# Residual of a token-mixing block: accumulating DMA into the output against loads and VectorE additions

## The chip, the core and the metric

The kernel runs on one core of one Trainium2 chip. The core has five engines with instruction queues of their own: TensorE (PE in the profile, with its weight loads shown apart as PEld), VectorE (DVE), ScalarE (ACT), GpSimd (POOL) and SyncE (SP). PE writes its results to PSUM; the other data lie in SBUF. DMA transfers between SBUF and the chip's memory are issued from the queues of SP, ACT or POOL and run on 16 DMA engines. The metric is device time in microseconds of one execution, given as the median of several runs.

## The reference, cut to what matters

```python
def reference(A_x, A_wqkv, A_wo, B_x, B_w1, B_b1, B_w2, B_b2):
    ...
    def _B_ref(x, w1, b1, w2, b2):
        h = _layernorm(x, axis=-1)
        u = jnp.einsum("bsd,sf->bdf", h, w1) + b1
        u = _gelu(u)
        y = jnp.einsum("bdf,fs->bds", u, w2) + b2
        return y.transpose(0, 2, 1)

    x = A_x
    h = x + _A_ref(_layernorm(x, axis=-1), A_wqkv, A_wo)
    h2 = h + _B_ref(_layernorm(h, axis=-1), B_w1, B_b1, B_w2, B_b2)
    return h2
```

_A_ref, left out here, is linear attention with 32 heads and a product with wo. The input is bf16 with S = 2048 tokens and D = 1024 channels. The first half adds linear attention to x and gives h. The second half mixes over the tokens: a product with w1 (2048 x 3584), a gelu, a product with w2 (3584 x 2048), a bias per token. Its result is added to h, the residual. This last addition, h + mixer, is what the change is about.

## The kernel before

The kernel has three stages. Attention runs up to about 235 us: projections, the key-value products, then for each of the NS = 16 blocks of 128 tokens the output projection (out_mm), which yields a block of h as a 128x1024 tile. out_evac (L1393) copies that block to SBUF as h_bf, takes its statistics for the layer norm, and stores it to a scratch tensor in memory, h_dram[i] (L1402). The normalized h stays in SBUF as the input of the mixer's first product; the plain h is needed again only at the very end.

The first mixer product (class Mixer1) and the second (class Mixer2) follow, the latter from about 390 us. Both use a seven-product scheme of Strassen's kind: instead of eight block products, seven products of sums and differences of blocks (methods p1 to p7) are accumulated in PSUM, and some of the seven are themselves taken apart once more in the same way (class Inner, methods i1 to i7). PE does the products; DVE makes the sums and differences of operands (tiles sa, is, gi, gs) and of partial results (e); ACT copies between PSUM tiles. psA, psB and psC are PSUM tiles of 128x512, psI one of 128x256.

A Mixer2 object with number p makes the blocks 2p and 2p + 1 of 128 tokens (sh = 0 or 1), each in two halves of CW = 512 channels (dh = 0 or 1). That gives 32 results of 128x512. Two Mixer2 objects at a time form a Quad, handled by run2, which interleaves the matmuls of one Quad with those that end the Quad before it: steps p4 of the earlier pair (result sh = 1, dh = 0) are filled in between the inner products of the next. The order of PE and DVE in this part is written out by hand: all instructions there keep program order (Held.on = True).

A result ends in Mixer2.out (L472). First either ACT (evac, from psA, psC or e) or DVE (evac_shared, from psC or psB with e added) writes the result with its bias to ot, an SBUF tile with three buffers. Then DVE adds hr, the block of h that fetch (L467) loaded from h_dram earlier, and SP stores ot to the output. hr has six buffers, and its 32 loads and the stores share SP's queue with the loads of w2 (load_w2, L160). [...]

The last Quad is called with cut = 384: the very last result is split into 384 and 128 columns (split), so that the work behind the last matmul is short.

Of the kernel before, what the change touches and what calls it, by code (L numbers as in the profile page):

```python
# [10 lines left out]
P = 128  # L11
F32 = mybir.dt.float32
BF16 = mybir.dt.bfloat16
FP16 = mybir.dt.float16
ACT = mybir.ActivationFunctionType
ALU = mybir.AluOpType
# [6 lines left out]
BANK = 512  # L23
XRL = 3
XR2 = 8
ACT_SET_LN_EXP = 6
SEED_RESIDUAL = True

# [2 lines left out]
def kernel(  # L31
# [12 lines left out]
    nc = tc.nc  # L44
    x = A_x.flatten_outer_dims()
    o_dram = out.flatten_outer_dims()
    S, D = x.shape
    F = B_w1.shape[1]
    NS, ND, NF = S // P, D // P, F // P
    CW = min(BANK, D)  # L50
# [147 lines left out]
            part()  # L198

    dram = ctx.enter_context(tc.tile_pool(name="dram", bufs=1, space=bass.MemoryType.DRAM))  # L200
    h_dram = [dram.tile([P, D], BF16, name=f"h_dram{i}") for i in range(NS)]
    sactx = ctx.enter_context(ExitStack())
    mctx = ctx.enter_context(ExitStack())

# [26 lines left out]
    dve, pe, act = Held(nc.vector), Held(nc.tensor), Held(nc.scalar, key="scalar")  # L231
    hv, ht, hs, hd = (Held(e, True) for e in (nc.vector, nc.tensor, nc.scalar, nc.sync))
# [222 lines left out]
    class Mixer2(Product7):  # L455
# [9 lines left out]
            return dve.tensor_tensor(t, self.a11, self.a21, ALU.subtract)  # L465

        def fetch(self, sh, dh):  # L467
            t = outp.tile([P, CW], BF16, tag="hr", bufs=6, name="hr")
            nc.sync.dma_start(t[:], h_dram[2 * self.p + sh][:, dh * CW:(dh + 1) * CW])
            self.hr[sh, dh] = t  # L470

        def out(self, sh, dh, a, b, op):  # L472
            i = 2 * self.p + sh
            ot = outp.tile([P, CW], BF16, tag="ot", bufs=3, name="ot")
            op(ot[:, a:b], b2_sb[:, i:i + 1])
            dve.tensor_tensor(ot[:, a:b], ot[:, a:b], self.hr[sh, dh][:, a:b], ALU.add)
            nc.sync.dma_start(o_dram[i * P:(i + 1) * P, dh * CW + a:dh * CW + b], ot[:, a:b])

        def evac(self, sh, dh, ps, a=0, b=CW):
            self.out(sh, dh, a, b, lambda ot, bias: nc.scalar.activation(  # L480
# [12 lines left out]
    def share(sts):  # L493
        t = cpool.tile([P, 2, BANK], F32, tag="e", name="e1")
        for s, st in enumerate(sts):
            st.e = t[:, s, :]
        return t[:]

    class Quad:
# [79 lines left out]
        def run2(self, pend, on_p4, on_p7, cut, third_sums):  # L579
            sts = self.sts  # L580

            def starting():
                self.in1.sums(slice(2, 4))
                self.asums(5)
                self.in5 = self.inner(5)
                self.in5.sums(slice(0, 2))
                sts[0].asum(6)
                for st in sts:
                    st.begin()

            self.interleave(
                self.in1, self.steps(*[st.p4 for st in pend]),
                {"b": starting, "7": lambda: self.in5.sums(slice(2, 4))}, (("b", self.early), ("7", None), ("end", None)),
            )
            sts[1].asum(6)
            on_p4()
            e = share(sts)
            for st in sts:
                st.fetch(1, 1)
            for st in sts:  # L600
                st.fetch(0, 0)
                st.fetch(0, 1)
            sts[0].asum(7)
            self.interleave(self.in5, self.steps(*[st.p6 for st in sts]))
            sts[1].asum(7)
            third_sums()
            self.asums(3)
            in3 = Inner2(sts, 3, self.mov3, "i", self.add_to(e), None)
            in3.sums()
            for st in sts:  # L610
                st.p7()
                dve.tensor_tensor(st.e[:], st.B[:], st.e[:], ALU.add)
            if cut is not None:
                sts[-1].split(cut)
            for st in sts:
                st.fetch(1, 0)
            nxt, halves = on_p7()

            def begin_next():
                if nxt is not None:  # L620
                    nxt.in1 = nxt.inner(1)
                    nxt.in1.sums(slice(0, 2))
                sts[0].evac(0, 1, sts[0].e)

            self.interleave(in3, self.steps(*[st.p2 for st in sts]), {
                "2": halves[0], "7": halves[1], "third": begin_next,
                "end": lambda: self.late.append(lambda: sts[1].evac(0, 1, sts[1].e)),
            }, (("7", None),))
            return sts, nxt
# [111 lines left out]
    with ExitStack() as actx:  # L741
# [21 lines left out]
        with ExitStack() as a1:  # L763
# [256 lines left out]
            def run_step(n, prev, after6=None, after5=None, after7=None, fill=None):  # L1020
# [34 lines left out]
            nc.scalar.add_instruction(  # L1055
                mybir.InstLoadActFuncSet(name=nc.get_next_instruction_name(), act_func_set_id=ACT_SET_LN_EXP, ins=[], outs=[])
            )
# [172 lines left out]
            for q in range(2, NVP):  # L1230
                for R in (KRun, VRun):
                    n = R(q)
                    i = 2 * q + 3 if R is KRun else 2 * q + 4
# [57 lines left out]
        with ExitStack() as a3:  # L1291
# [41 lines left out]
            def den_spread(u):  # L1333
                rows = rd_dram[u].rearrange("(g o h) n -> o h g n", g=4, h=HB)
                for h in range(2):
                    rdb = a3d.tile([P, NH, SW], FP16, tag="rdb", bufs=3, name="rdb")
                    for q in range(HB):
                        hd.dma_start(
                            rdb[q * DH:(q + 1) * DH, :, :],
                            rows[h, q].unsqueeze(0).to_broadcast([DH, 4, SW]),  # L1340
                        )
                    rdbs[u, h] = rdb

            def den(u):
                den_inv(u, den_mm(u))
# [21 lines left out]
            def load_xr(i):  # L1367
                if i < NS:
                    pool = xr2pool if XRL < i <= XRL + XR2 else xrpool
                    xr = pool.tile([P, D], BF16, name="xr")  # L1370
                    hd.dma_start(xr[:], x[i * P:(i + 1) * P, :])
                    xrs[i] = xr
# [20 lines left out]
            def out_evac(i):  # L1393
                ps = seeds.pop(i)
                h_bf = a3w.tile([P, D], BF16, name="h_bf")
                h_bfs[i] = h_bf
                st = a3s.tile([P, NDC, nc.vector.BN_STATS_DIM], F32, name="hst")
                for dc in range(NDC):
                    hs.copy(h_bf[:, dc * CW:(dc + 1) * CW], ps[dc][:, 0:CW])
                    hv.bn_stats(st[:, dc, :], ps[dc][:, 0:CW])  # L1400
                hv.bn_aggr(mv_all[:, i, :], st[:])
                hd.dma_start(h_dram[i][:], h_bf[:])  # L1402

            def h_scale(i):
                lnv = a3s.tile([P, 1], F32, name="hln_l")
# [47 lines left out]
            a3w = a3.enter_context(tc.tile_pool(name="a3w", bufs=4))  # L1453
            xr2pool = a3.enter_context(tc.tile_pool(name="xr2pool", bufs=XR2))

# [7 lines left out]
            for i in range(NS):  # L1463
                seed(i + 1)
                out_mm(i)
                if i == 0:
                    load_xr(XRL + 1)
                    den(NSC - 1)
                    for k in range(XRL + 2, XRL + XR2 + 1):
                        load_xr(k)  # L1470
                if i == 2:
                    den_spread(NSC - 1)
                if i < NS - XRL - XR2 - 1:
                    load_xr(i + XRL + XR2 + 1)
                if i == NS - 1:
# [37 lines left out]
    def next_load1(u):  # L1513
        def load():
            if u < NQ1:
                load_w1(u, 0)
                load_w1(u, 1)
            else:
                first_w2(0)
        return load  # L1520

    def quad1(u):
        return Quad([Mixer1(2 * u), Mixer1(2 * u + 1)], mov1, mov5, mov2, mov3)
# [4 lines left out]
    pend, nxt = cur.run_first(quad1(1), sums1, sums2)  # L1528
    for u in range(1, NQ1):
        cur = nxt  # L1530
        pend, nxt = cur.run1(pend, lambda: quad1(u + 1) if u + 1 < NQ1 else None, next_load1(u + 1), sums3 if u == 1 else None)
# [11 lines left out]
    outp = ctx.enter_context(tc.tile_pool(name="outp", bufs=1, side="right", reuse_waits="tile"))  # L1543
# [46 lines left out]
    def run_all(fs):  # L1590
        for f in fs:
            f()

    def after_p4(u):
        def act():
            run_all(make_t3)
            for p in (2 * u + 2, 2 * u + 3):
                if 4 <= p < NSP:
                    load_w2(p, 1)
        return act  # L1600

    def next2(u):
        for p in (2 * u, 2 * u + 1):
            load_w2(p, 0)
        return quad2(u)

    def after_p7(u):
        return lambda: (next2(u + 1) if 2 * u + 2 < NSP else None, make_t4)

    pend = [cur, Mixer2(1)]  # L1610
    share(pend)
    for st in pend:
        st.fetch(0, 0)
        st.fetch(1, 1)
        st.fetch(0, 1)
    for st in pend:
        if st is pend[1]:
            for m in (5, 6, 7):
                st.asum(m)
            run_all(make_t3_raw)  # L1620
        st.p1()
        st.p5()
        if st is not pend[1]:
            st.p2()
        st.p6()
# [2 lines left out]
    sums5()  # L1628
    for st in pend:
        st.p7()  # L1630
    for st in pend:
        st.fetch(1, 0)
    nxt = next2(1)
    nxt.early = 0
    run_all(make_t4)
# [6 lines left out]
    for u in range(1, NSP // 2):  # L1642
        cur = nxt
        pend, nxt = cur.run2(
            pend, after_p4(u), after_p7(u), CW - P if 2 * u + 2 == NSP else None, sums3 if u == 1 else nop,
        )
# [34 lines left out]
```

## Time and profile before

| What | us |
|---|---|
| median of 5 runs | 563.05 |
| lowest to highest | 562.69 to 563.22 |
| the profiled execution, its own time | 562.69 |
| its span in the profile | 560.9 |
| end of the first part, start of the second mixer product | about 390 |
| start of the last unbroken run of matmuls (42 on psC) | 551.31 |
| last store issued | 558.2 |

The span is what the profiler saw from the first to the last instruction; the execution's own time is 1.8 us more. The profile numbers instructions by line of the source (L229 is a helper through which most of the recorded instructions pass, so the names of tiles tell them apart). In a timeline, a line is a run of like instructions: start, length, engine, line, operation, output and inputs, how many; in brackets stands how long the engine had been idle before, and what it waited for. Matmul ends are modelled, so starts are the safer measure.

The rows of DMA issues that concern the residual, with the size of one and the median time from issue to landing:

```profile
h_dram<-h_bf SPq DMA_DIRECT2D x16, 256.0 KB, 2.0
hr<-h_dram SPq DMA_DIRECT2D x32, 128.0 KB, 2.9
out_dram<-ot SPq DMA_DIRECT2D x31, 128.0 KB, 1.9
```

The core's clock was full throughout (a granted TensorE clock of 1.00 in every stretch).

### The profile page before, as it was taken

What the parts mean: (1) busy time and instruction counts of PE and PEld (TensorE: products, weight loads), DVE (VectorE), ACT (ScalarE), POOL (GpSimd) and SP (SyncE); (2) the same over time, 40 slices, a digit from 0 to 9 for tenths busy, and PEclk for the clock granted to TensorE, in tenths of its full rate; (3) what the DMA queues carried; (4) which work ended last, traced back from release to release, by engine and by line L of the source; (5) the groups of instructions that cost most, each with busy time, mean ns of one, the idle gap of its engine ahead of it and who ended that gap; (6) DMA issues with size and microseconds to landing.
All of it is one profiled execution on the core that took longest, in us unless ns stands there. A gap on an engine that the chain in (4) does not pass through costs nothing.

```text
span 560.9 us, 8720 instructions
## 1 busy us (share of the span) xinstructions
PE 554.0 (99%) x3260; PEld 309.6 (55%) x3276; DVE 447.5 (80%) x853; ACT 288.6 (51%) x611; POOL 1.8 (0%) x8
## 2 busy tenths in 40 slices
PE   8999999999999999999999999999999999999997
PEld 3444444454444444456666766666445655656654
DVE  7898888544776788889989789888998889879874
ACT  5647777756766877645546465564211313313212
POOL 1000000000000000000000000000000000000000
PEclk9999999999999999999999999999999999999999
DMA  9933332115765851103141340422946643642111
GB/s 304 299 74 76 88 82 39 19 56 190 215 192 146 264 178 76 75 1 110 43 150 28 124 151 1 151 70 63 237 134 193 169 110 115 189 134 94 56 39 56
DMA packets 86217, 67.15 MB, mean 120 GB/s; under 512 B 15890, under 2 KB 80160, under 8 KB 86176
## 3 DMA queue, kind: packets, MB, share of 16 engines
q1 hardware_dynamic: 85440, 65.94, 40.2%
q10 hardware_dynamic: 672, 0.66, 0.4%
q8 instruction: 25, 0.41, 0.3%
q14 instruction: 16, 0.13, 0.1%
q0 software_dynamic: 64, 0.01, 0.0%
HBM read 54.54 MB, written 8.91 MB: 113 GB/s over the span
## 4 chain that ended last, share of the span: by engine, by line
PE 91%; DVE 5%; DMA 1%; issue 1%; SPq 0%; ACT 0%; DVEq 0%
PE psI L229 21%; PE acc_t L229 18%; PE psC L229 14%; PE psB L229 8%; PE psC L907 4%; PE psB L907 4%; PE psA L907 4%; PE psA L229 3%; PE psB L341 2%; PE psA L341 2%; PE acc_t L1193 2%; PE psE L907 2%; PE psC L341 2%; PE acc_t L831 2%; DMA x_sb<-in_A_x_dram 1%; PE kvps L860 1%
## 5 line engine op out<-in xcount | busy, mean ns | idle before, releaser
L229 PEld LDWEIGHTS <-is 128*128 128x128 f16 x652 | 63.7, 98 | 29.3 <-issue 0.9
L229 PEld LDWEIGHTS <-sa 128*128 128x128 f16 x606 | 59.3, 98 | 28.3 <-issue 0.4
L229 PEld LDWEIGHTS <-wq 128*128 128x128 bf16 (+1 forms) x503 | 49.2, 98 | 32.9 <-issue 1.0
L229 PE MATMUL acc_t<-wo_sb,pqT 128*128 128x512 f16 x256 | 55.6, 379 | 0.0
L229 PE MATMUL acc_t<-xnT,wq_sb 128*128 128x512 bf16 x188 | 43.1, 379 | 0.2
L229 PEld LDWEIGHTS <-pqT 128*128 128x128 bf16 x256 | 25.0, 98 | 30.5 <-issue 0.6
L191 DVE TENSOR_SCALAR e_sb<-e_sb 128x512 bf16<-128x512 bf16 x64 | 18.5, 290 | 28.8 <-ACT e_sb L187 28.2
L187 ACT ACTIVATE e_sb<-acc_t 128x512 bf16<-128x512 f32 x40 | 23.9, 597 | 24.5 <-PE acc_t L229 12.0
L907 PEld LDWEIGHTS <-xs 128*128 128x128 f16 x208 | 20.0, 98 | 23.4 <-DVE xs L893 1.3
L229 PE MATMUL psC<-gs,wq 128*128 128x512 f16 x140 | 32.0, 379 | 0.0
L229 PE MATMUL psC<-hT,sa 128*128 128x512 f16 x112 | 31.2, 379 | 0.0
L229 PEld LDWEIGHTS <-wq_sb 128*128 128x128 bf16 x192 | 18.5, 98 | 23.0 <-issue 1.3
L229 PE MATMUL psI<-hi,is 128*128 128x256 f16 x200 | 30.0, 273 | 0.0
L229 PE MATMUL psB<-hT,sa 128*128 128x512 f16 x112 | 29.7, 379 | 0.0
L229 DVE BATCH_NORM_STATS2 hst<-acc_t 128x6 f32<-128x512 f32 x32 | 21.4, 692 | 9.1 <-ACT h_bf L229 8.9
L907 PE MATMUL psA<-wkv,xnT 128*128 128x512 bf16 x99 | 26.4, 379 | 0.3
L907 PEld LDWEIGHTS <-xnT 128*128 128x128 bf16 x156 | 15.2, 98 | 18.5 <-issue 0.2
L229 PE MATMUL psC<-hT,wq 128*128 128x512 f16 x96 | 24.6, 379 | 0.0
L229 ACT CAST h_bf<-acc_t 128x512 bf16<-128x512 f32 x32 | 18.4, 581 | 12.0 <-PE acc_t L229 12.0
L229 ACT COPY psI<-psI 128x256 f32<-128x256 f32 x50 | 18.0, 360 | 11.7 <-PE psI L229 9.8
L188 ACT ACTIVATE r_sb<-acc_t 128x512 bf16<-128x512 f32 x40 | 23.7, 593 | 0.0
L831 PE MATMUL acc_t<-wkv,xnT 128*128 128x512 bf16 x94 | 21.6, 379 | 0.2
(225 smaller groups left out, 1074.4 us busy)
## 6 DMA issues: line engine op xcount, KB each, us to landing
wq<-in_B_w_dram SPq DMA_DIRECT2D x14, 1024.0 KB, 7.9
wq<-in_B_w_dram SPq DMA_DIRECT2D x12, 896.0 KB, 5.9
xr<-in_A_x_dram SPq DMA_DIRECT2D x16, 256.0 KB, 5.5
rdb<-rd_dram SPq DMA_DIRECT2D x32, 128.0 KB, 3.9
h_dram<-h_bf SPq DMA_DIRECT2D x16, 256.0 KB, 2.0
hr<-h_dram SPq DMA_DIRECT2D x32, 128.0 KB, 2.9
out_dram<-ot SPq DMA_DIRECT2D x31, 128.0 KB, 1.9
x_sb<-in_A_x_dram SPq DMA_DIRECT2D x15, 256.0 KB, 3.1
```

The costliest lines, as they stand in the source:

```text
L187: pin(nc.scalar.activation(e_sb[:], src, ACT.Exp))
L188: pin(nc.scalar.activation(r_sb[:], src, ACT.Relu))
L191: pin(nc.vector.tensor_scalar(e_sb[:], e_sb[:], 1.0, PHI_EPS, ALU.min, ALU.add))
L229: return (lambda *a, **kw: pin(op(*a, **kw))) if self.always or getattr(Held, self.key) else op
L341: pe.matmul(ps[:, cols], lhsT=lhs[:, k, :], rhs=mv(k)[:, cols], start=(start and k == 0), stop=(k == self.nk - 1), skip_group_check=True,)
L831: mm = nc.tensor.matmul(pp[:, 0:CW], lhsT=xnT[:, kt, i * P:(i + 1) * P], rhs=wkv[:, kt, c * CW:(c + 1) * CW], start=(kt == 0), stop=(kt == ...
L860: pin(nc.tensor.matmul(kv_ps[b][:, sl, :], lhsT=pks[i % NPK][:, j * P:(j + 1) * P], rhs=vaugs[i % NVA][:, j, :], start=False, stop=(i == N ...
L907: pin(nc.tensor.matmul(ps[:], lhsT=lhs[:, k, :], rhs=rhs[:, k, :], start=(start and k == 0), stop=(k == hk2 - 1), skip_group_check=True,))
L1193: nc.tensor.matmul(qp[:, 0:SW], lhsT=wq_sb[:, kt, j * P:(j + 1) * P], rhs=xnT[:, kt, u * SW:(u + 1) * SW], start=(kt == 0), stop=(kt == ND ...
```

## The change

The scratch tensor goes. The first half stores its blocks of h to the output tensor itself. In the second mixer product, a result for which no h was loaded is written to ot with its bias as before, and then added to what stands in the output by a DMA with an accumulating write, issued from POOL's queue. DVE's addition and the load of h fall away for these. For the last Quad alone (cut is given), the results sh = 1, dh = 0 of its two objects still load h, from the output, and take the old way. ot has four buffers in place of three, hr two in place of six.

```diff
+OTB = 4
...
-    h_dram = [dram.tile([P, D], BF16, name=f"h_dram{i}") for i in range(NS)]
...
         def fetch(self, sh, dh):
-            t = outp.tile([P, CW], BF16, tag="hr", bufs=6, name="hr")
-            nc.sync.dma_start(t[:], h_dram[2 * self.p + sh][:, dh * CW:(dh + 1) * CW])
+            t = outp.tile([P, CW], BF16, tag="hr", bufs=2, name="hr")
+            i = 2 * self.p + sh
+            nc.sync.dma_start(t[:], o_dram[i * P:(i + 1) * P, dh * CW:(dh + 1) * CW])
             self.hr[sh, dh] = t
 
         def out(self, sh, dh, a, b, op):
             i = 2 * self.p + sh
-            ot = outp.tile([P, CW], BF16, tag="ot", bufs=3, name="ot")
+            ot = outp.tile([P, CW], BF16, tag="ot", bufs=OTB, name="ot")
             op(ot[:, a:b], b2_sb[:, i:i + 1])
-            dve.tensor_tensor(ot[:, a:b], ot[:, a:b], self.hr[sh, dh][:, a:b], ALU.add)
-            nc.sync.dma_start(o_dram[i * P:(i + 1) * P, dh * CW + a:dh * CW + b], ot[:, a:b])
+            to = o_dram[i * P:(i + 1) * P, dh * CW + a:dh * CW + b]
+            if (sh, dh) in self.hr:
+                dve.tensor_tensor(ot[:, a:b], ot[:, a:b], self.hr[sh, dh][:, a:b], ALU.add)
+                nc.sync.dma_start(to, ot[:, a:b])
+            else:
+                nc.gpsimd.dma_start(to, ot[:, a:b], accum_op=ALU.add)
...
             e = share(sts)
-            for st in sts:
-                st.fetch(1, 1)
-            for st in sts:
-                st.fetch(0, 0)
-                st.fetch(0, 1)
...
-            for st in sts:
-                st.fetch(1, 0)
+            if cut is not None:
+                for st in sts:
+                    st.fetch(1, 0)
...
-                hd.dma_start(h_dram[i][:], h_bf[:])
+                hd.dma_start(o_dram[i * P:(i + 1) * P, :], h_bf[:])
...
     share(pend)
-    for st in pend:
-        st.fetch(0, 0)
-        st.fetch(1, 1)
-        st.fetch(0, 1)
...
-    for st in pend:
-        st.fetch(1, 0)
     nxt = next2(1)
```

## The prediction

> **What bounds the kernel now.** I read the page's busy times first, then the chain of waits over the second mixer (390 us to the end), then TensorE's (PE's) timeline there, because an addition on VectorE (DVE) is worth only what PE gets from it.
>
> ```profile
> PE 554.0 (99%) x3260; PEld 309.6 (55%) x3276; DVE 447.5 (80%) x853; ACT 288.6 (51%) x611; POOL 1.8 (0%) x8
> ```
>
> The next lines are windows: start and end, length, then busy time of PE, PEld, DVE, ACT, POOL.
>
> ```profile
> 430.00:470.00 40.00, 39.62 (x251) 24.37 (x250) 35.71 (x48) 8.94 (x21) 0.00 (x0) 1.00 0.49 138
> 470.00:510.00 40.00, 39.89 (x258) 25.23 (x258) 32.88 (x48) 10.88 (x24) 0.00 (x0) 1.00 0.51 145
> 510.00:550.00 40.00, 40.00 (x260) 25.25 (x258) 32.86 (x47) 11.04 (x25) 0.00 (x0) 1.00 0.16 51
> ```
>
> PE is busy nearly throughout; DVE has some 7 us free in each 40. The instructions' order on PE and ACT is the same before and after, so PE's work stays and only its gaps can close. I looked for gaps between matmul starts from 385 us to the end. A 512-column matmul takes 216 ns from start to start (7 in 1.51 us in the chain), and only three intervals are over 260 ns, all near 465 us:
>
> ```profile
> 462.75 1.67 PE L229 MATMUL psA<-gO,w2o 128*128 128x512 f16 x7
> 464.42 0.92 PE L229 MATMUL psI<-gO,is 128*128 128x256 f16 x7
> 465.94 1.24 PE L229 MATMUL psA<-gO,w2o 128*128 128x512 f16 x5
> 467.51 0.92 PE L229 MATMUL psI<-gO,is 128*128 128x256 f16 x7 [0.32 <-DVE e L229]
> 468.27 1.67 PE L229 MATMUL psA<-gO,w2o 128*128 128x512 f16 x7
> 470.11 0.92 PE L229 MATMUL psI<-gi,sa 128*128 128x256 f16 x7 [0.17 <-DVE e L229]
> ```
>
> Expected start after 462.75 is 462.75 + 7 x 0.216 = 464.26, found 464.42: 0.15 lost. After 465.94 it is 467.02, found 467.51: 0.49. After 468.27 it is 469.78, found 470.11: 0.33. Together 0.97 us, the whole idle time of PE in the changed part. Each of these matmuls starts just after DVE has read the PSUM tile psI into e, and DVE has been the chain from 450.40 on:
>
> ```profile
> 461.29 0.42 DVE L229 TENSOR_TENSOR ot<-ot,hr 128x512 bf16<-128x512 bf16 x1
> 461.63 0.68 DVE L229 TENSOR_TENSOR e<-psB,e 128x512 f32<-128x512 f32 x1
> 463.00 0.42 DVE L229 TENSOR_TENSOR ot<-ot,hr 128x512 bf16<-128x512 bf16 x1
> 463.35 0.68 DVE L229 TENSOR_TENSOR e<-psB,e 128x512 f32<-128x512 f32 x1
> 463.95 0.41 DVE L229 TENSOR_TENSOR e<-psI,e 128x256 f32<-128x256 f32 x1
> 467.37 0.41 DVE L229 TENSOR_TENSOR ot<-ot,hr 128x512 bf16<-128x512 bf16 x1
> ```
>
> Three of the additions that the change removes stand in that stretch.
>
> **What the Trainium skill says.** "DMA: Bandwidth & Descriptors", section "SWDGE vs HWDGE vs iDMA": an accumulating DMA can only be issued from GpSimd, whose cores write its descriptors in software; the trace has no accumulating DMA. The same page, "Anatomy of one DMA", prices one such DMA at about 2.0 us plus bytes over 436 GB/s: for 128 KB an estimate of 2.3 us. The two small bias loads on POOL landed 4.7 and 5.4 us after issue, above that, but amid the loads of the start. "SBUF — State Buffer", section "Who interferes with whom": tensor_tensor has no mode that takes both ports, and contends only with a GpSimd operation that reads SBUF. Nearly all of DVE's work in this part is tensor_tensor, so descriptor writing and DVE should leave each other alone. No run here shows it.
>
> **The change part by part.** Before, 32 results of 128x512 (the last cut in two) get h from loads and additions. After, 30 go by accumulating DMA as the built program lists them; the left halves of row blocks 13 and 15 (pieces of 512, 384 and 128 columns) still take a loaded h.
>
> *DVE.* 30 additions of 0.42 us go: 12.6 us busy, and most of the 10.0 us that DVE waits on ACT in front of eight of them. In the tight stretch, an addition holds the next instruction by 0.34 us (461.29 to 461.63; 463.00 to 463.35; 467.37 to 467.70). The addition to e behind the first two now waits on DVE's own result itself, so I credit 0.34 and not 0.42. Before the first gap that makes 0.68, against the 0.15 lost. The two reads of psI at 466.21 then end near 466.6 (the matmuls they need end by 466.0), against PE's unstalled need at 467.51 - 0.15 - 0.49 = 466.87: the second gap goes with 0.3 to spare. With the third addition 1.0 is saved; DVE's next read of psI would end near 468.9, needed at 470.11 - 0.97 = 469.14: the third goes with 0.2 to spare. Gain 0.97 us. The other 27 additions stand beside a PE without gaps: nothing. What is late next is PE itself.
>
> *SP.* 30 loads of h (0.42 us of issue) and 30 stores (0.34) leave the queue. The weight loads behind them (L161) wait for their own buffers: those at 417.79 and 420.82 follow the ends of PE's psC stretches (414.74 to 420.79), so they don't start earlier. Nothing.
>
> *DRAM.* The first mixer's 16 stores of h keep size, queue and place, with the output as target: nothing. An accumulate must read what is there, so 30 loads plus 30 stores of 128 KB become about the same traffic. The DMA share here is about 0.5, falling to 0.16 after 510. A weight load that lands late has 2.4 us of cover at the one DVE wait (landing 427.2, used by PE at 429.7). Nothing.
>
> *POOL.* It does nothing after 3 us, so 30 issues have it to themselves. Each waits for its result, an old store of h and a semaphore of eight DMAs ago; only further accumulates stand behind it. Descriptor time g: the bias loads took 0.67 us (28 rows) and 0.51 (16), 13 ns a row, hence 2.0 for 128 rows if it grows so and 0.6 if it doesn't; I take 1.5. From descriptors to landing, D: 1.5 from the output stores of before, 4.2 from the bias loads less their issue; I take 2.8, the page's 2.3 and an estimated half microsecond for reading the destination.
>
> *Buffers.* ot has four buffers, so a result waits for the accumulate four results earlier. These are mostly over 8 us apart (470.72 against 461.3, 554.53 against 545.43 + 0.69), against g + D = 4.3. At the end they are close:
>
> ```profile
> 550.51 0.72 ACT L480 ACTIVATE ot<-e,b_sb 128x512 bf16<-128x512 f32 x1 [4.39 <-DVE e L229]
> 551.14 0.67 ACT L480 ACTIVATE ot<-psA,b_sb 128x512 bf16<-128x512 f32 x1
> 552.06 0.72 ACT L480 ACTIVATE ot<-e,b_sb 128x512 bf16<-128x512 f32 x1 [0.25 <-DVE e L229]
> 554.53 0.69 ACT L480 ACTIVATE ot<-psC,b_sb 128x512 bf16<-128x512 f32 x1 [1.75 <-PE psC L229]
> 556.81 0.58 ACT L480 ACTIVATE ot<-psC,b_sb 128x384 bf16<-128x384 f32 x1 [1.59 <-PE psC L229]
> 557.59 0.37 ACT L480 ACTIVATE ot<-psC,b_sb 128x128 bf16<-128x128 f32 x1 [0.20 <-PE psC L229]
> ```
>
> The last line (128 columns) reuses the buffer of the second (psA). Shifted by the gain, the first is ready at 551.23 - 0.97 = 550.26; two accumulates in a row land at about 550.36 + 2g + D = 556.2, and the buffer is wanted at 556.6. Cover 0.4. The third lands at 550.36 + 3g + D = 557.7, before the last store (issued 558.24, 1.5 to landing, less 0.97: 558.8). So the tail (ACT, addition of h, store) keeps its length.
>
> Sum against the profiled execution: 562.69 (span 560.9 and 1.8 around it) - 0.97 = 561.7. The runs' median is 0.36 above that execution: 563.05 - 0.97 = 562.1.
>
> **The rivals.**
> 1. *Slower: accumulates queue at the end.* If 2g + D exceeds 6.24 the last piece waits; from 7.2 on the 0.97 is eaten up. With g = 2.0 and D = 4.5 the landing is 558.9, 2.3 after 556.6: net +1.3, 564.3. For it: the slope of the bias loads and their slow landing. Against: those shared the engines with the start's loads; the end is quiet (DMA 0.19).
> 2. *Slower: descriptor writing blocks DVE.* Two accumulates start between 461 and 464, where DVE is the chain. If each holds DVE for 1.0 us, DVE loses 2.0 and saves 1.0, and PE's gaps grow by about 1.0: 564.1. Elsewhere DVE's free time absorbs it. Against: the skill's rule above.
> 3. *No change: the gaps stay.* The margins of 0.2 and 0.3 are small; if the read of psI is delayed otherwise, only the first gap and part of the second go: 0.4 us, 562.65.
> That the change does not do what it says is excluded: 30 accumulates stand on POOL's queue.
>
> **How the numbers follow.** A difference under 0.2%, 1.1 us, is no change to this measurement. The forecast, 562.1 (own range 561.8 to 562.5), has 0.55; it lies 0.2 short of that bound, 561.92, so I split it 0.34 faster, 0.21 within. Rival 1: 0.18 (0.12 slower, 0.06 within). Rival 2: 0.14 (0.11 slower, 0.03 within). Rival 3: 0.13, of which 0.02 faster. Sums: faster 0.36, within 0.41, slower 0.23. The range is 561.6 to 564.4: 561.6 because PE has no more to give than 0.97 beyond scatter (0.5 between the runs shown), 564.4 to take in both slower rivals' prices.
>
> **What would show it.** Right: no interval over 260 ns between matmul starts near 465 us, DVE some 12 us less busy, the span about 1 us shorter with 3.3 us from PE's last matmul to the end as now. Rival 1: the last ACT result waits for a DMA on POOL's queue. Rival 2: longer DVE instructions or idle time just as POOL issues. I would be wrong outright if PE lost time where it has no gap now.

## The result, and the profile after

The changed kernel takes 561.95 us (median of 23 runs, 561.58 to 564.52) against 563.0 us for the kernel before (43 runs, 562.57 to 564.65). The ratio is 0.9985 with a 95% interval of 0.9979 to 0.9992: 0.85 us faster, between 0.45 and 1.2 (the two medians differ by 1.05). The forecast was 562.1, a gain of 0.97. Two of the medians below, 562.99 and 564.93, include one execution of over 900 us each; without it they are 562.96 and 564.78, and the ratios leave it out.

The execution that was profiled first happened to start late: PE waited 1.9 us for a weight load near 8 us and reached the mixer's first matmul 2.9 us behind the kernel before, so its span is 562.7. Some runs of the kernel before are as long (564.65). A second profile of the same kernel (run e11_after_again below) starts like the kernel before and has a span of 560.1. All profiles of "the changed kernel" here are that one. Its page, busy times (first part) and DMA queues (third part), the latter as packets, MB and share:

```profile
PE 553.8 (99%) x3260; PEld 309.7 (55%) x3276; DVE 437.6 (78%) x823; ACT 288.6 (52%) x611; POOL 27.9 (5%) x38
...
q1 hardware_dynamic: 76800, 58.07, 35.6%
q0 software_dynamic: 4384, 3.95, 5.5%
...
HBM read 50.61 MB, written 8.91 MB: 106 GB/s over the span
```

DVE has 30 instructions fewer and 9.9 us less busy time: 30 times about 0.33 us, since successive DVE instructions overlap in the records and 0.42 is counted only in part. POOL now has 38 instructions and 26 us more. Queue q0, POOL's, carries 3.95 MB, nearly all of it the 30 results of 128 KB.

PE's timeline at the place of the three gaps:

```profile
462.91 1.67 PE L229 MATMUL psA<-gO,w2o 128*128 128x512 f16 x7
464.42 0.93 PE L229 MATMUL psI<-gO,is 128*128 128x256 f16 x7
...
465.95 1.24 PE L229 MATMUL psA<-gO,w2o 128*128 128x512 f16 x5
467.03 0.93 PE L229 MATMUL psI<-gO,is 128*128 128x256 f16 x7
467.79 1.67 PE L229 MATMUL psA<-gO,w2o 128*128 128x512 f16 x7
469.30 0.93 PE L229 MATMUL psI<-gi,sa 128*128 128x256 f16 x7
```

462.91 + 7 x 0.216 = 464.42, 465.95 + 5 x 0.216 = 467.03, 467.79 + 7 x 0.216 = 469.30: each matmul starts when the one before is through. No interval from 390 us to the end exceeds 260 ns. From the mixer's first matmul (psA from hE) to the last matmul of all, the kernel before took 323.58 us and the changed one 322.62: 0.96 us, the gain. From the last matmul's start to the end of the span, called the tail below, it is 3.54 before and 3.53 after.

DVE's timeline in the same stretch shows how narrowly the gaps closed:

```profile
465.70 1.24 DVE L229 TENSOR_TENSOR e<-psI,e 128x512 f32<-128x512 f32 x2
...
468.79 0.42 DVE L229 TENSOR_TENSOR e<-psI,e 128x256 f32<-128x256 f32 x1
```

The two reads of psI end at 465.70 + 1.24 = 466.94, 0.09 us before PE starts; the last ends at 469.21, again 0.09. In the kernel before, PE did wait for these same reads:

```profile
466.21 1.24 DVE L229 TENSOR_TENSOR e<-psI,e 128x512 f32<-128x512 f32 x2
...
469.64 0.42 DVE L229 TENSOR_TENSOR e<-psI,e 128x256 f32<-128x256 f32 x1
```

They end at 467.45 and 470.06, and PE started at 467.51 and 470.11, 0.05 to 0.06 later. So of the 0.09 us about 0.03 is reserve.

### The profile page after: what moved, and what is told of

It reads as the page before. It is cut to its first block, busy times and chain, and to the rows that moved or that the text cites. A ratio compares the mean times of both kernels' runs of the same rounds, so it can differ in the third digit from the quotient of the medians.

```text
span 562.7 us, 8633 instructions
## 1 busy us (share of the span) xinstructions
PE 555.1 (99%) x3260; PEld 310.2 (55%) x3276; DVE 437.5 (78%) x823; ACT 288.5 (51%) x611; POOL 28.0 (5%) x38
## 3 DMA queue, kind: packets, MB, share of 16 engines
q0 software_dynamic: 4384, 3.95, 5.6%
HBM read 50.61 MB, written 8.91 MB: 106 GB/s over the span
## 4 chain that ended last, share of the span: by engine, by line
PE 96%; DMA 1%; DVE 1%; ACT 1%; issue 0%; ACTq 0%
PE psI L229 22%; PE acc_t L229 18%; PE psC L229 16%; PE psB L229 8%; PE psA L229 4%; PE psC L908 4%; PE psB L908 4%; PE psA L908 4%; PE acc_t L832 3%; PE psB L341 2%; PE psA L341 2%; PE acc_t L1194 2%; PE psE L908 2%; PE psC L341 2%; DMA wkv<-in_A_wqkv_dram 1%; PE kvps L861 1%
## 5 line engine op out<-in xcount | busy, mean ns | idle before, releaser
L482 POOL DMA_DIRECT2D out_dram<-ot x30 | 26.1, 906 | 526.8 <-ACT ot L485 452.6
L229 DVE TENSOR_TENSOR e<-psI,es 128x256 f32<-128x256 f32 x20 | 8.5, 425 | 22.1 <-PE psI L229 22.1
L832 PE MATMUL acc_t<-wkv,xnT 128*128 128x512 bf16 x94 | 23.1, 398 | 2.0 <-DMA wkv<-in_A_wqkv_dram 1.9
```

Of the source, the lines that this page charges most:

```text
L229: return (lambda *a, **kw: pin(op(*a, **kw))) if self.always or getattr(Held, self.key) else op
L482: nc.gpsimd.dma_start(to, ot[:, a:b], accum_op=ALU.add)
L832: mm = nc.tensor.matmul(pp[:, 0:CW], lhsT=xnT[:, kt, i * P:(i + 1) * P], rhs=wkv[:, kt, c * CW:(c + 1) * CW], start=(kt == 0), stop=(kt == ...
```

## The experiments

Two questions were open. Is the whole gain these three gaps? And what does the accumulating DMA cost, and where? Times are medians in us; the ratio is to the kernel before, measured on the same chip, with its 95% interval.

### Three additions put back

```diff
+TIGHT = ((2, 1, 1), (3, 1, 1), (2, 0, 0))
...
                 nc.gpsimd.dma_start(to, ot[:, a:b], accum_op=ALU.add)
+                if (self.p, sh, dh) in TIGHT:
+                    junk = outp.tile([P, CW], BF16, tag="junk", bufs=1, name="junk")
+                    dve.tensor_tensor(junk[:], ot[:], ot[:], ALU.add)
```

> The changed kernel, with a DVE addition of the old size (128x512 bf16, result unused) put back behind three of the 30 accumulated results, those whose additions stood between 461 and 468 us. If the gain is PE's three gaps near 465 us, these three additions bring all of them back: about 0.97 us more than the changed kernel, 563.0, with three matmul intervals of about 0.37, 0.70 and 0.55 us there. If the gain comes from all 30 additions together, or from SP's shorter queue, a tenth of it comes back: 562.0 to 562.1.

Measured: 562.99, ratio 0.9998 (0.9990 to 1.0006). The intervals between matmul starts near 465 us are 0.370, 0.704 and 0.546 us, against 0.370, 0.703 and 0.545 in the kernel before. PE's timeline of this run:

```profile
466.04 1.24 PE L230 MATMUL psA<-gO,w2o 128*128 128x512 f16 x5
467.61 0.92 PE L230 MATMUL psI<-gO,is 128*128 128x256 f16 x7 [0.33 <-DVE e L230]
468.37 1.67 PE L230 MATMUL psA<-gO,w2o 128*128 128x512 f16 x7
470.21 0.93 PE L230 MATMUL psI<-gi,sa 128*128 128x256 f16 x7 [0.17 <-DVE e L230]
```

Three additions out of 30 take the whole gain back.

### Only these three accumulated

```diff
         def fetch(self, sh, dh):
-            t = outp.tile([P, CW], BF16, tag="hr", bufs=2, name="hr")
+            if (self.p, sh, dh) in TIGHT:
+                return
+            t = outp.tile([P, CW], BF16, tag="hr", bufs=6, name="hr")
...
+            for st in sts:
+                st.fetch(1, 1)
+            for st in sts:
+                st.fetch(0, 0)
+                st.fetch(0, 1)
```

The other calls of fetch stand where they stood before as well.

> The converse: only these three results go by accumulating DMA; the other 29 load h (from the output, six hr buffers) and are added on DVE as before. If the three gaps are the whole gain, it is all here: 562.0, no PE interval over 260 ns near 465 us. If the other 27 additions, or the 54 transfers that leave SP's queue, carry the gain, the time stays at about 562.9.

Measured: 562.12, ratio 0.9983 (0.9973 to 0.9992). No matmul interval over 260 ns, and 322.62 us from the mixer's first matmul to the last. With the run above this settles where the gain is: 27 additions, and the loads and stores that leave SP's queue, are worth nothing that can be measured.

### No residual at all

```diff
-                nc.gpsimd.dma_start(to, ot[:, a:b], accum_op=ALU.add)
+                nc.sync.dma_start(to, ot[:, a:b])
...
-                    st.fetch(1, 0)
+                    pass
```

> Leaves out the addition of h: results go to the output by plain stores on SP, with no loads of h, no DVE additions and no accumulating DMA. It asks what the accumulates cost. If PE is the bound and the accumulates run beside it at no cost, it saves only the last piece's addition (about 0.25 us): 561.7. If descriptor writing, the accumulates' traffic or their landing at the end cost something, it is faster by that much: 561.0 or less.

Measured: 561.86, ratio 0.9977 (0.9971 to 0.9984). The matmuls take 322.62 us as in the changed kernel; the tail is 3.34 instead of 3.53, the missing last addition. So beside PE the 30 accumulates cost nothing that shows.

### Each POOL transfer doubled

```diff
                 nc.gpsimd.dma_start(to, ot[:, a:b], accum_op=ALU.add)
+                nc.gpsimd.dma_start(dram.tile([P, CW], BF16, name=f"again{i}_{dh}")[:, a:b], ot[:, a:b])
```

> Each accumulate is followed on POOL's queue by a plain store of the same tile to a scratch tensor, so POOL writes descriptors for 60 transfers instead of 30 and ot is held longer. If descriptor writing held DVE, the stretch near 465 us gets twice as much of it, and PE's gaps return: over 563. If not, only the end can suffer: five of six descriptor writings of 0.9 us before the last piece's buffer is free, landing at about 550.4 + 5 x 0.9 + 2.8 = 557.7 against 556.6: 562.0 to 563.0, with no PE gap near 465.

Measured: 562.46, ratio 0.9995 (0.9986 to 1.0004). POOL's timeline in the tight stretch, then DVE's:

```profile
463.01 0.94 POOL L482 DMA_DIRECT2D out_dram<-ot  x1
463.57 0.94 POOL L483 DMA_DIRECT2D again<-ot  x1
465.09 0.87 POOL L482 DMA_DIRECT2D out_dram<-ot  x1 [0.59 <-ACT ot L486]
465.65 0.87 POOL L483 DMA_DIRECT2D again<-ot  x1
```

```profile
463.69 2.02 DVE L229 TENSOR_TENSOR gs<-gO,gT 128x3584 f16<-128x3584 f16 x1
465.62 1.24 DVE L229 TENSOR_TENSOR e<-psI,e 128x512 f32<-128x512 f32 x2
```

POOL writes descriptors while DVE works on gs, and gs takes 2.02 us as in the kernel before. No gap in PE. Descriptor writing does not hold these DVE instructions. The time falls in the range I gave, but not for the reason I gave: the last ACT result began at 556.75, right after its matmuls, so no buffer was late. The 0.5 us are lost after the last store, which the next two experiments explain.

### The last pieces accumulated too

```diff
                 for st in sts:
-                    st.fetch(1, 0)
+                    pass
```

> The last three pieces go by accumulating DMA too. It prices an accumulate on the path that sets the end. Now: addition 0.23, issue on SP 0.34, landing 1.5 after issue. With an accumulate: 0.86 of descriptor writing within 3.7 from issue to landing: about 3.7 - 0.23 - 1.5 = 2.0 us more, less a little as the 128-column piece is smaller: 563.5 to 564.0. If accumulates are as quick as stores at the quiet end, 562.0 or less.

Measured: 564.93, ratio 1.0027 (1.0018 to 1.0035), 2.8 to 3.0 over the changed kernel where 1.6 to 2.1 were expected. The tail is 6.10 us instead of 3.53, and two parts make up the difference of 2.56. First, the last packet ended at 560.2 and SP had seen every transfer landed at 560.93, 4.20 us after the start of the last matmul, against 2.76 in the changed kernel: 1.45 us, close to what was expected of the accumulates. The other 1.1 us are lost after that. The span ends at 562.8, and what ran until 562.0 is POOL's own closing instruction, a drain. Its row in this run (durations in ns as minimum, median, maximum, then first and last start):

```profile
L1671 POOLq DRAIN  x3: 46/102/4366, 557.7 to 562.5; - x3
```

The 4366 ns one starts at 557.7 and ends at 562.03, 3.15 us after POOL finished its last descriptors at 558.88. In the doubled run the drain ended at 559.77 while SP was through at 559.21: those are its 0.56 us.

```profile
L1672 POOLq DRAIN  x3: 51/102/7166, 552.6 to 560.3; - x3
```

### The last piece stored, not accumulated, from POOL

```diff
-                nc.sync.dma_start(to, ot[:, a:b])
+                (nc.gpsimd if b - a == P else nc.sync).dma_start(to, ot[:, a:b])
```

> The changed kernel, but the plain store of the very last 128-column piece is issued from POOL's queue instead of SP's; no accumulate is added. It tells what made the all-accumulate kernel 3.0 us slower than the changed one. If it is POOL's closing drain, which ended 3.2 to 5.1 us after POOL's last descriptor writing in the runs so far, the end moves here too: piece ready, 0.9 of descriptor writing, at least 3.2 of drain, 0.7 to the span's end = 4.8, against 2.6 from the last addition to the end now: 563.9 to 564.9. If only accumulating is slow to land, a plain store costs at most POOL's longer way to landing, 2.9 against 1.5: 562.8 to 563.3.

Measured: 563.83, ratio 1.0015 (1.0008 to 1.0021), 1.8 over the changed kernel on the same chip (561.99). The row of the drain here and, in the second fence, in the changed kernel:

```profile
L1671 POOLq DRAIN  x3: 51/102/3346, 557.8 to 561.6; - x3
```

```profile
L1671 POOLq DRAIN  x3: 51/102/4676, 552.2 to 559.8; - x3
```

The plain store landed 1.8 us after issue, SP was through at 559.74, and the drain ended at 561.13: the drain set the end. Of the tail's 1.8 us more, 0.4 is the later landing (SP is through 3.16 us after the last matmul's start instead of 2.76) and 1.4 the drain. The time lies just under the range given for the drain (563.9), because descriptors took 0.57 instead of 0.86 and the drain 2.8 after them instead of 3.2. In the changed kernel the long drain ends at 556.84 and SP is through at 559.29, so the drain is hidden, with 2.4 us to spare. Keeping the last three pieces off POOL is what hides it.

### Fewer ot buffers

```diff
-OTB = 4
+OTB = 3
```

> Three ot buffers instead of four. The last piece then waits for the third of the three accumulates in a row at the end, the 384-column piece for the second. They landed by 1.2 us or more before these pieces were wanted (queue 0's last packet ended 1.5 us before the last ACT result began), so nothing moves: 562.0. If the fourth buffer is needed, 562.5 or more.

Measured: 562.01, ratio 0.9974 (0.9966 to 0.9983). The fourth buffer is not needed. With two:

> Two ot buffers in place of four. A result then waits for the accumulate two results earlier, 3.7 us from issue to landing. Where three results come within 2 us (near 471, 512 and 552 us), the third waits some 2.6 us, and the ACT copy of psI that PE needs stands behind it in ACT's queue: twice 2.5 us of PE gap, and some 3.4 us at the end: about 570. If results leave soon enough, or ACT's free time covers it, 562.

Measured: 563.7, ratio 1.0015 (1.0007 to 1.0023). My 570 was far off. ACT's timeline shows why, near the first of the three places:

```profile
470.74 0.69 ACT L485 ACTIVATE ot<-psA,b_sb 128x512 bf16<-128x512 f32 x1 [0.49 <-DMA out_dram<-ot]
471.33 0.38 ACT L269 COPY psI<-psI 128x256 f32<-128x256 f32 x1
473.67 0.72 ACT L485 ACTIVATE ot<-e,b_sb 128x512 bf16<-128x512 f32 x1 [1.97 <-DMA out_dram<-ot]
```

ACT does wait for accumulates, 0.49 and 1.97 us, as expected. But with two buffers the built order has the psI copy ahead of the waiting result, where the other kernels have it behind (470.77, then 471.40 in the changed kernel). PE has no gap; only the end pays, with a tail of 5.25 us instead of 3.53.

### A shorter tail, and the changed kernel beside it

```diff
         def evac(self, sh, dh, ps, a=0, b=CW):
+            if (sh, dh) in self.hr:
+                i = 2 * self.p + sh
+                ot = outp.tile([P, CW], BF16, tag="ot", bufs=OTB, name="ot")
+                dve.scalar_tensor_tensor(ot[:, a:b], ps[:, a:b], b2_sb[:, i:i + 1], self.hr[sh, dh][:, a:b], ALU.add, ALU.add)
+                nc.sync.dma_start(o_dram[i * P:(i + 1) * P, dh * CW + a:dh * CW + b], ot[:, a:b])
+                return
```

> The last three pieces are made by one DVE instruction each (PSUM plus bias plus h) in place of ACT and then a DVE addition. Behind the last matmul, 0.38 (ACT) and 0.23 (DVE) with a hand-over become one DVE instruction of about 0.3: 0.3 us less, 561.6. If the end is set by something else (stores on SP, accumulates on POOL), no change: 561.95.

Measured: 561.67, ratio 0.9985 (0.9968 to 1.0002). The interval is wide, so it was measured again, beside the changed kernel:

> The kernel with the fused last three pieces once more, on one chip with the changed kernel itself. The tail behind the last matmul was 3.18 us against 3.52: 0.34 us faster than the changed kernel, 561.6, and under the kernel before by 1.3 us. If the first measurement was scatter, the two are equal.

> The changed kernel itself, unedited, beside the other three: 561.95 as before. Its profiled execution should show the start of the kernel before (first matmul of the mixer at about 233.8 us instead of 236.6) and a span of about 559.9 us; if the late start seen in its first profile belongs to the change, it starts late again.

Measured: 561.64, ratio 0.9974 (0.9967 to 0.9981), and for the changed kernel 561.99, ratio 0.9979 (0.9972 to 0.9986). The two intervals overlap, but both pairs of medians differ by 0.3 and both tails by 0.35 (3.18 in the two runs, against 3.53). DVE's last instruction in the fused kernel:

```profile
556.69 0.35 DVE L229 SCALAR_TENSOR_TENSOR ot<-psC,b_sb,hr 128x128 bf16<-128x128 f32 x1 [0.16 <-PE psC L229]
```

One instruction of 0.35 replaces ACT's 0.37 and DVE's 0.22 with a hand-over between them. This version is the fastest of the kernels tried. The late start did not come back in e11_after_again, and the kernel before has executions as long (564.65, 565.06); nothing ties it to the change.

## Why the prediction was right, step by step

- **The gain is PE's three gaps.** Right, in place and in size: 0.97 forecast, 0.96 in the traces, and shown from both sides by putting three additions back and by leaving only three out. The measured 0.15% lies within the 0.2% that the prediction took as no change, the outcome to which it gave the largest chance (0.41); a second measurement gives 0.21% (0.14 to 0.28%).
- **The other 27 additions, SP's queue and h's new place cost or bring nothing.** Right: three accumulates alone bring the gain, and with three additions put back it is gone, though h's new place, the shorter SP queue and all 30 accumulates remain.
- **Margins of 0.3 and 0.2 us in DVE's schedule.** Wrong in size. I had the two reads of psI end near 466.6, but 467.45 less the two savings of 0.34 is 466.77; I had the last near 468.9, but 470.06 less three savings is 469.04. That leaves 0.10 in both places, and I left out the 0.05 to 0.06 from DVE's end to PE's start. The measured reserve is about 0.03 us. Closing the second and third gaps in full was therefore closer to luck than the prediction said: any delay of DVE over 0.03 us in that stretch would have reached PE.
- **DVE 12.6 us less busy.** It was 9.9, or 0.33 per addition: the 0.34 of the tight stretch was the right figure here too, not 0.42.
- **POOL: g = 1.5, D = 2.8.** g was 0.86 for a single accumulate and up to 1.18 in a row, with starts as little as 0.58 apart; the row of DMA issues has 3.6 from issue to landing, so D = 2.7. The slope taken from the two bias loads was no guide to 128 rows, and these loads give a D of 4.0 and 4.9 (4.67 less 0.67, 5.43 less 0.51), not 4.2. That D came out near 2.8 is partly luck: the half microsecond for reading the destination was worked out from nothing. The buffers were free well before they were wanted: queue q0's last packet ended at 555.2, the last ACT result began at 556.84.
- **The tail keeps its length.** Right (3.54 and 3.53), but the sum lacked a term: POOL's closing drain, which happened to end 2.4 us before it could matter. Rival 1 looked for the danger at ot's buffers; where POOL works late (each transfer doubled, or a last piece sent from POOL), the runs show it at the drain.
- **Rival 2, descriptors block DVE.** Refuted for this mix of DVE instructions: twice the descriptor writing left gs at 2.02 us and PE without a gap. This agrees with the Trainium skill, "SBUF — State Buffer", section "Who interferes with whom", which has tensor_tensor contend only with what GpSimd reads from SBUF.
- **About the same traffic.** The memory's read counter fell from 54.54 to 50.61 MB, by the 30 loads. It shows 50.34 MB both with all results accumulated and with no residual at all, so an accumulate's read of its destination is not in this counter; what it is in bytes stays open.

## What to carry to other kernels

When one engine is full, add up the gaps between its instructions' starts in the stretch that a change touches: that sum, not the work removed from a neighbour, is what the change can bring. Here 3 of 30 removed additions carried everything: of 9.9 us taken off DVE, 0.96 reached the time. An accumulating DMA can take an addition off a busy engine where the result leaves anyway and POOL is idle: the 30 here cost POOL 26 us and PE nothing that shows. The last transfers are better kept off POOL, as far as these runs go: one small store from POOL at the end cost 1.8 us.

## What was not expected of the hardware

POOL's closing drain ends well after POOL's last descriptor writing: 2.8 us with one small store last, 3.15 with accumulates last, 3.8 in the changed kernel, 5.1 with six transfers in a row last. On the page of the changed kernel it shows in no wait and no busy time, only as a row of POOL's queue.

Part of this is the last transfer's way to landing. What remains behind the landing differs between the runs, and their traces show a pattern:

| Kernel | POOL's transfers in all | from the last landing to the drain's end, us |
|---|---|---|
| kernel before (two bias loads) | 2 | 0.12 |
| only three accumulated | 5 | 0.25 |
| changed kernel | 32 | 1.35 |
| last piece stored from POOL | 33 | 1.57 |
| all accumulated | 35 | 1.48 |
| each transfer doubled | 62 | 2.93 |

The more transfers POOL had issued in the whole kernel, the later the drain ended: some 0.04 to 0.06 us per transfer. In the first two kernels POOL stops early and the drain runs in the middle of the work, so this is a pattern over runs that differ in other ways too. No run changed the number alone, and why the drain takes this time stays open. With three accumulates it ended 2.3 us after the last descriptor writing, so the lower end of 3.2 us that was expected above did not hold for all runs made by then.
